# FFN1 by seven block products over two tiles, with Q, K, V plain: one kernel, one core

## The chip, the cores and the metric

The kernel runs on one core of one Trainium2 chip. The metric is the device time of one execution in microseconds; lower is better. The engines are TensorE (PE in the profile, its weight loads PEld), VectorE (DVE), ScalarE (ACT), GpSimd (POOL) and SyncE (SP), which here only issues DMAs. Each engine runs its own instructions in the order in which the built program holds them; semaphores order the engines among themselves.

## The reference

```python
def _A_ref(x, wqkv, wo):                      # S = 2048, D = 576, H = 32, Dh = 18
    qkv = (x @ wqkv).reshape(B, S, 3, H, Dh).transpose(2, 0, 3, 1, 4)
    q, k, v = qkv[0], qkv[1], qkv[2]
    idx = pos[:, None] - off[None, :]         # 8 keys, two apart, behind each position
    mask = idx >= 0
    ...
    logits = jnp.einsum("bhsd,bhswd->bhsw", q, kg) * Dh ** -0.5
    logits = jnp.where(mask[None, None, :, :], logits, -1e9)
    o = jnp.einsum("bhsw,bhswd->bhsd", _softmax(logits, axis=-1), vg)
    return o.transpose(0, 2, 1, 3).reshape(B, S, D) @ wo

def _B_ref(x, w1, b1, w2, b2):                # F = 4608
    h = jnp.einsum("bsd,df->bsf", x, w1) + b1
    r = jnp.where(h > 0, h, 0)
    return jnp.einsum("bsf,fd->bsd", r * r, w2) + b2

xn = _layernorm(A_x, axis=-1)
return A_x + _A_ref(xn, A_wqkv, A_wo) + _B_ref(xn, B_w1, B_b1, B_w2, B_b2)
```

## The kernel before, in words

The 2048 positions are four tiles (`b`) of 512. The model dimension 576 is four chunks of 128 rows and a leftover of 64; the 4608 hidden features are 36 blocks (`f`) of 128. Every factor of a matmul is held as a rounded high part and the difference to it (`split`, L142 to L146: ScalarE writes the high part, DVE the difference), and a product is made of high x high, high x low and low x high. The leftover's two parts are stacked in one chunk of 128 rows.

One loop runs over 144 steps `n`, that is 36 blocks for each tile in turn (`step`). A step loads the weights of a later block, splits the w1 block of the next step (`split_w1`) and its own w2 block (`split_w2`, L149 and L150), runs FFN1 of block `n` (`ffn1`, L698: 14 matmuls of 512 columns into one bank), then ScalarE's relu (L700) and two squares (L703, L704) and DVE's difference (L705), and FFN2 of block `n - 2` (`ffn2`, L723: 14 matmuls into the tile's five output banks). So FFN2 uses activations that were made two steps earlier. At a tile's end the output projection (65 matmuls, also L723) goes into the same banks, and DVE drains them (`drain`, L739) onto the residual.

Around that go, as pieces between the steps: layer norm of the next tile (statistics on DVE, L161 to L169, the inverse root on GpSimd, L170, mean and scale through DRAM by two DMAs named `mr` and `mb`, then L358), Q, K, V, and the attention of eight heads at a time (`attention`): products and sums over DVE (L626, L629), a softmax, and the weighted values, whose sum over the window of eight is three halving additions (L652 to L654). K and V go through DRAM, which shifts them.

Q, K, V of tile 0 are plain matmuls, 14 for each group of 128 rows (L259 in the opening, L404 later). Tiles 2 and 3, and half of tile 1, take them by seven block products over two halves of the rows, the columns and the inner chunks (`multiply`, L586). GpSimd makes the combined weights for that in advance (`preparation`) and passes them through DRAM (`wm`, `we`).

The opening (`open_rows`) loads tile 0 row by row, normalises and transposes it, multiplies its first group of Q, K, V, and goes straight on to FFN1 of block 0. On TensorE, ScalarE, DVE and GpSimd the order of the opening is the order of the code; later the planner of the framework places each engine's instructions, except the last step.

Of the kernel before, what the change touches and what calls it, by code (L numbers as in the profile page):

```python
# [16 lines left out]
P = 128  # L17
# [6 lines left out]
NF = F // P  # L24
G = 4
HG = H // G
CG = HG * DH
HALO = (W - 1) * DIL
# [8 lines left out]
LAG = 2  # L37
WARM = 6
WQ, KV = 512, 2688
WIDE = (448, 512, 384, 384)  # L40
QAT = [sum(n - 2 * CG for n in WIDE[:g]) for g in range(G + 1)]
PAIR = (512, 352)
QP = (0, 448)
PREP = {(1, 0): range(6, 13), (1, 1): (31, 32, 32, 33, 34, 34, 35, 37, 38, 38), (0, 0): range(40, 47), (0, 1): range(51, 61)}
HOME = {(1, 0): "xr", (1, 1): "xb", (0, 0): "xr", (0, 1): "xr"}
OUTS = {}
LEAD = {6: 1, 7: 1, 5: 1, 3: 1}
LN, XT, NORM, RES = {1: 22, 2: 20, 3: 18}, {1: 25, 2: 15, 3: 14}, {1: 12, 2: 9, 3: 11}, {1: 28, 2: 13, 3: 13}
PRODUCTS = {1: {1: range(6, 13)}, 2: {0: range(-6, 1), 1: range(3, 10)}, 3: {0: range(-6, 1), 1: range(3, 10)}}
FETCH = {1: ((2, 14), (3, 18)), 2: ((0, 1), (1, 6), (2, 11), (3, 16)), 3: ((0, 1), (1, 6), (2, 11), (3, 16))}  # L50
PLAIN = {1: ((0, -6, -2), (1, 1, 4))}
# [3 lines left out]
def block_kernel(ctx: ExitStack, tc: tile.TileContext, x, xt, wqkv, wpair, wo, w1, b1, w2, b2, out):  # L55
# [4 lines left out]
    py = ctx.enter_context(tc.tile_pool(name="py", bufs=1, space=bass.MemoryType.PSUM))  # L60
    pw = ctx.enter_context(tc.tile_pool(name="pw", bufs=1, space=bass.MemoryType.PSUM))
# [6 lines left out]
    ident = sb.tile([P, P], F32, name="mb", bufs=1)  # L68
# [6 lines left out]
    zero = sb.tile([PAD, CG], F32, name="pr", bufs=1)  # L75
# [11 lines left out]

    kscr = [dram.tile([PAD + S, CG], F32, name=f"kscr{g}") for g in range(G)]
    vscr = [dram.tile([PAD + S, CG], F32, name=f"vscr{g}") for g in range(G)]

# [3 lines left out]

    oscr = {(b, g): dram.tile([TB, CG], F32, name=f"o{b}{g}") for b in range(NB) for g in range(G)}
    mrscr = {b: dram.tile([2 * NJ, P], F32, name=f"mr{b}") for b in range(1, NB)}

    normed, mb = {0}, {}
    xb, xT, xr, xh, xl, qo, ob, wq = {}, {}, {}, {}, {}, {}, {}, {}
    raw1, raw2, w1s, w2s, hs = {}, {}, {}, {}, {}  # L100
    yp = {}
    turns, held = [0], set()

    def bank(own=False):
        turns[0] += not own
        if own or turns[0] % 3 == 0:
            return pw.tile([P, TB], F32, name="wk")
        return pw.tile([P, TB], F32, name="qk", bufs=2)

    wm = [[dram.tile([P, 4, n], F32, name=f"wm{p}{i}") for i in range(7)] for p, n in enumerate(PAIR)]  # L110
    we = [[dram.tile([P, 2, n], F32, name=f"we{p}{i}") for i in range(3)] for p, n in enumerate(PAIR)]

    def load_x(b, j):
        if b not in xb:
            xb[b] = sb.tile([P, NJ, D], F32, name="xb", bufs=1)
        with tc.issue_after(last_load[0].ins):
            nc.sync.dma_start(xb[b][:, j], xv[b][:, j])

    def load_xt(b):
        xT[b] = sb.tile([P, NC, TB], F32, name="xt", bufs=1)  # L120
        with tc.issue_after(last_load[0].ins):
            nc.sync.dma_start(xT[b], xt[b])

    def load_first():
        xb[0] = sb.tile([P, NJ, D], F32, name="xb", bufs=1)
        raw = sb.tile([P, NC, TB], F32, name="xr", bufs=1)[:, :, :WIDE[0]]
        hi = mt.tile([P, NC, WQ], F32R, name="wqh")[:, :, :WIDE[0]]
# [86 lines left out]
    def open_rows():  # L214
# [13 lines left out]
        def stats(j, *ks):  # L228
            for k in ks:
                bn_stats(0, j, k)  # L230
# [770 lines left out]
```

## Time and profile before

| | before |
|---|---|
| median of three runs | 1150.9 us (1150.66 to 1150.94) |
| span of the profiled execution | 1148.8 us |
| TensorE busy | 1143.9 us, 5167 matmuls |
| DVE busy | 896.9 us |
| ScalarE busy | 598.3 us |
| GpSimd busy | 167.8 us |
| DMA | 244.32 MB, 213 GB/s over the span |

The span goes from the first to the last instruction of one execution taken by the hardware profiler. Rows of groups give line, engine, operation, output <- inputs, shapes and count, then the busy time in us, the mean of one in ns, and the engine's idle time just before them with what ended it. Rows of the chain of waits and of the timeline begin with the start and the length in us. The ends of matmuls are modelled and overlap, so the pitch of matmuls is read from start to start.

### The profile page before, as it was taken

To read this page: it belongs to the slowest core of one execution; us is meant where nothing else is said; L and a number is where in the kernel's file an instruction comes from. 1 tells how busy PE (TensorE), PEld (TensorE's weight loads), DVE (VectorE), ACT (ScalarE), POOL (GpSimd) and SP (SyncE) were. 2 spreads that over 40 slices of the span, in tenths; PEclk is the share of its full clock that TensorE was granted. 3 is DMA by queue.
4 is the path that set the end of the run, shared out by engine and by line. 5 is a ranking of instruction groups with operands and counts; after the bars stand their busy time and mean duration, and the time that the engine had idled before them with its cause. 6 is when DMAs were issued, how large, how long until landed. Compare 5 with 4: busy or idle time off the path is not lost.

```text
span 1148.8 us, 14771 instructions
## 1 busy us (share of the span) xinstructions
PE 1143.9 (100%) x5167; PEld 956.6 (83%) x5167; DVE 896.9 (78%) x1314; ACT 598.3 (52%) x1010; POOL 167.8 (15%) x233
## 2 busy tenths in 40 slices
PE   9999999999999999999999999999999999999998
PEld 7888888888888888888888888888888888888887
DVE  6878898973598999996558899989555989998453
ACT  7646455563545546566335445556543544555652
POOL 2232100012245316420100100000100010000000
PEclk9999999999999999999999999999999999999999
DMA  7749576553679798897578598563667868643421
GB/s 247 247 137 333 141 255 208 151 158 106 227 236 339 224 317 262 272 307 227 181 268 296 184 341 275 144 185 119 192 209 276 283 189 270 216 124 108 133 68 53
DMA packets 102506, 244.32 MB, mean 213 GB/s; under 512 B 14080, under 2 KB 36608, under 8 KB 97184
## 3 DMA queue, kind: packets, MB, share of 16 engines
q1 hardware_dynamic: 86096, 185.20, 50.4%
q0 software_dynamic: 16048, 57.81, 15.7%
q8 instruction: 40, 0.66, 0.2%
q10 hardware_dynamic: 288, 0.38, 0.1%
q14 instruction: 34, 0.28, 0.1%
HBM read 209.34 MB, written 34.00 MB: 212 GB/s over the span
## 4 chain that ended last, share of the span: by engine, by line
PE 99%; DMA 0%; DVE 0%; POOL 0%; issue 0%; POOLq 0%
PE y L723 45%; PE wk L698 20%; PE qk L698 20%; PE qk L586 8%; PE qk L404 3%; PE wk L404 2%; PE qk L259 1%; PE y L195 0%; DMA xb<-in_x 0%; PE wk L259 0%; DVE st L161 0%; PE qk L773 0%; PE wk L773 0%; POOL rs L170 0%; DVE xr L775 0%; DVE xt L189 0%
## 5 line engine op out<-in xcount | busy, mean ns | idle before, releaser
L723 PE MATMUL y<-hh,w2s 128*128 128x512 f32 x1292 | 323.3, 389 | 0.0
L723 PEld LDWEIGHTS y<-hh,w2s 128*128 128x128 f32 x1292 | 242.3, 188 | 49.3
L143 ACT ACTIVATE w1h<-raw 128x640 fp32r<-128x640 f32 x144 | 106.3, 739 | 186.8 <-PE wk L698 102.3
L723 PE MATMUL y<-hl,w2s 128*128 128x512 f32 x718 | 190.3, 389 | 0.0
L145 DVE TENSOR_TENSOR w1l<-raw,w1h 128x640 fp32r<-128x640 f32 x144 | 121.8, 846 | 77.8 <-ACT w1h L143 40.7
L149 ACT ACTIVATE w2s<-raw 128x640 fp32r<-128x640 f32 x144 | 105.8, 737 | 146.1 <-PE y L723 135.7
L723 PEld LDWEIGHTS y<-hl,w2s 128*128 128x128 f32 x718 | 134.7, 188 | 27.6
L150 DVE TENSOR_TENSOR w2s<-raw,w2s 128x576 fp32r<-128x576 f32 x144 | 115.5, 803 | 45.9 <-ACT w2s L149 45.3
L705 DVE TENSOR_TENSOR hl<-r,hh 128x512 fp32r<-128x512 f32 x144 | 103.5, 719 | 31.4 <-ACT r L704 31.0
L698 PE MATMUL wk<-xh,w1h 128*128 128x512 f32 x360 | 106.0, 390 | 0.0
L698 PE MATMUL qk<-xh,w1h 128*128 128x512 f32 x360 | 105.0, 389 | 0.0
L626 DVE TENSOR_TENSOR pr<-qo,kv 128x1152 f32<-128x1152 f32 x64 | 88.8, 1387 | 11.4 <-DMA kv<-kscr 7.6
L703 ACT ACTIVATE hh<-r 128x512 fp32r<-128x512 f32 x144 | 91.0, 632 | 4.9
L698 PE MATMUL wk<-xh,w1l 128*128 128x512 f32 x360 | 93.3, 389 | 0.0
L698 PE MATMUL qk<-xh,w1l 128*128 128x512 f32 x360 | 93.3, 389 | 0.0
L704 ACT ACTIVATE r<-r 128x512 f32<-128x512 f32 x144 | 90.9, 631 | 4.1
L648 DVE TENSOR_TENSOR pr<-lg,kv 128x1152 f32<-128x1152 f32 x64 | 88.7, 1385 | 1.2
L629 DVE TENSOR_REDUCE lg<-pr 128x64 f32<-128x1152 f32 x64 | 86.2, 1347 | 0.1
L698 PEld LDWEIGHTS wk<-xh,w1l 128*128 128x128 f32 x360 | 67.6, 188 | 14.1
L698 PEld LDWEIGHTS qk<-xh,w1l 128*128 128x128 f32 x360 | 67.6, 188 | 14.0
L698 PEld LDWEIGHTS qk<-xh,w1h 128*128 128x128 f32 x360 | 67.6, 188 | 13.9
L698 PEld LDWEIGHTS wk<-xh,w1h 128*128 128x128 f32 x360 | 67.3, 188 | 13.2
(176 smaller groups left out, 1560.1 us busy)
## 6 DMA issues: line engine op xcount, KB each, us to landing
raw<-in_w SPq DMA_DIRECT2D x288, 320.0 KB, 3.7
kv<-kscr SPq DMA_DIRECT2D x10, 1296.0 KB, 7.7
kv<-vscr SPq DMA_DIRECT2D x10, 1296.0 KB, 8.2
wqh<-wm POOLq DMA_DIRECT2D x12, 704.0 KB, 5.7
wqh<-wm POOLq DMA_DIRECT2D x8, 1024.0 KB, 5.8
raw<-in_wo SPq DMA_DIRECT2D x20, 320.0 KB, 3.1
wql<-wm POOLq DMA_DIRECT2D x9, 704.0 KB, 6.9
wql<-wm POOLq DMA_DIRECT2D x6, 1024.0 KB, 5.2
```

Of the source, the lines that this page charges most:

```text
L143: i = nc.scalar.activation(hi, raw, AF.Copy)
L145: i = nc.vector.tensor_tensor(out=lo, in0=raw, in1=hi.bitcast(F32), op=ALU.subtract)
L149: nc.scalar.activation(w[:, :DE], raw, AF.Copy)
L150: nc.vector.tensor_tensor(out=w[:, DE:], in0=raw[:, :D], in1=w[:, :D].bitcast(F32), op=ALU.subtract)
L586: nc.tensor.matmul(qk[t][:, :n], l, r, start=first and c == 0, stop=c == len(mm) - 1, skip_group_check=True)
L626: nc.vector.tensor_tensor(out=pr, in0=q[:, j:j + 1].to_broadcast([P, W, CG]), in1=shifted(k, j, [1, CG]), op=ALU.mult)
L648: nc.vector.tensor_tensor(out=pr.rearrange("p w (a d) -> p w a d", d=DH), in0=at[:, :, :, None].to_broadcast([P, W, HG, DH]), in1=shifted( ...
L698: nc.tensor.matmul(p, l, r, start=i == 0, stop=i == len(mm) - 1)
L703: nc.scalar.activation(hh, r, AF.Square)
L704: last_square[0] = nc.scalar.activation(r, r, AF.Square)
L705: last_hl[0] = nc.vector.tensor_tensor(out=hl, in0=r, in1=hh.bitcast(F32), op=ALU.subtract)
L723: nc.tensor.matmul(yp[b][c], v, a, start=first and c not in cs[:i], stop=c in last and c not in cs[i + 1:], skip_group_check=True)
```

## The change

FFN1 is computed for two tiles and two blocks of features at once. With the tiles `b0`, `b1` as the two rows of a block matrix, the chunks 0 and 1 against 2 and 3 as its inner halves, and the feature blocks 2p and 2p+1 as its columns, the four products that were eight half-products become seven (`ffn_pair`): B11, T1, T2, T3, B21, B22 and T4, each of six matmuls, with eight matmuls for the leftover chunk. T1 to T4 are differences of weight blocks that DVE makes for each pair (`combine_w1`); S1 to S4 are sums of activations that DVE makes once for each pair of tiles (`sums`, `last_sum`). Three banks carry the seven products (a, b, c in the text, `ba`, `bb`, `bc` in the code): ScalarE copies a to b after B11, T2 and T3 add onto b and ScalarE copies b out after each, and DVE adds such a copy to bank c.

The kernel then has four phases after an opening that computes Q, K, V of tiles 0 and 1 (`q0`). Phase A of tiles 0 and 1: 18 pairs of FFN1, with FFN2 of tile 0 (28 matmuls of the pair before) in four groups of seven between the products (`work`); tile 1's activations are written to DRAM (`hscr`), 1 MB a pair. Phase B of tile 1: FFN2 alone, 36 steps, with the activations read back (`load_h`), and the row products of Q, K, V of tiles 2 and 3 between its steps. Then phase A and phase B of tiles 2 and 3. Q, K, V are plain everywhere, 14 matmuls of 432 columns for each of the four groups of heads and each 128 rows. The seven products of Q, K, V, with `preparation` and its DRAM buffers, are gone. Attention's sum over the window is one reduction. TensorE's order is the order of the code throughout; attention is marked as work of low priority (`lazily`) that the planner sets between.

```diff
-    def preparation(p, m):
-    def multiply(b, p, i):
-    def ffn1(n):
...
-            nc.vector.tensor_tensor(out=pr[:, :4], in0=pr[:, :4], in1=pr[:, 4:], op=ALU.add)
-            nc.vector.tensor_tensor(out=pr[:, :2], in0=pr[:, :2], in1=pr[:, 2:4], op=ALU.add)
-            nc.vector.tensor_tensor(out=q[:, j], in0=pr[:, 0], in1=pr[:, 1], op=ALU.add)
+            nc.vector.tensor_reduce(out=q[:, j], in_=pr.rearrange("p w c -> p c w"), axis=AX.X, op=ALU.add)
...
+    def combine_w1(n):
+        r = raw1[n]
+        tt(r[:, T1:T3 + 1], r[:, B12:B22 + 1], r[:, B11:B12 + 1], ALU.subtract)
+        tt(r[:, T2], r[:, B22], r[:, T1], ALU.subtract)
+        tt(r[:, T4], r[:, B21], r[:, T2], ALU.subtract)
+
+    def split_w1(n, k):
+        w1s[n, k] = mt.tile([P, 2, 4, 2 * P], F32R, name="w1s", bufs=3)
+        split(w1s[n, k][:, 0], w1s[n, k][:, 1], raw1[n][:, 4 * k:4 * k + 4])
...
+        def product(to, slot, a, start=False, stop=False, extra=()):
+            mm = []
+            for c in range(2):
+                mm += [(weight(slot, 0, c), a(0, c))]
+            for c in range(2):
+                mm += [(weight(slot, 1, c), a(0, c)), (weight(slot, 0, c), a(1, c))]
+            for f, v in extra:
+                mm += [(weight(LEFT, k, f), v) for k in range(2)]
...
+        def squares(r, name_h):
+            h = mt.tile([P, 2, 2, TB], F32R, name="h", bufs=3)
+            nc.scalar.activation(h[:, 0], r, AF.Square)
+            nc.scalar.activation(r, r, AF.Square)
+            tt(h[:, 1], r, h[:, 0].bitcast(F32), ALU.subtract)
+            return h
+
+        product(ba, B11, A11, start=True)
+        if p == 0:
+            nc.tensor.matmul(bb, weight(B11, 0, 0), A11(0, 0), start=True, stop=True, skip_group_check=True)
+        nc.scalar.activation(bb, ba, AF.Copy)
+        product(bc, T1, ss(1), start=True)
+        work(0)
+        product(bb, T2, ss(2))
+        u = four()
+        nc.scalar.activation(u[:, 0], bb, AF.Copy)
+        left(bc, 1, x4[b1])
+        work(1)
+        product(bb, T3, ss(3))
+        nc.scalar.activation(u[:, 1], bb, AF.Copy)
+        r0, r1 = four(), four()
+        tt(r1[:, 1], bc, u[:, 1], ALU.add)
+        if p + 1 < NP:
+            combine_w1(n + 1)
+            split_w1(n + 1, 0)
+        product(ba, B21, A12, extra=((0, x4[b0]),))
+        relu(r0[:, 0], ba, f0)
+        relu(r1[:, 1], r1[:, 1], f1)
+        work(2)
+        product(bc, B22, S4, extra=((1, x4["d"]),))
+        tt(r0[:, 1], bc, u[:, 0], ALU.add)
+        relu(r0[:, 1], r0[:, 1], f1)
+        hs[n] = squares(r0, 0)
+        product(bb, T4, A22, extra=((0, x4[b1]),))
+        relu(r1[:, 0], bb, f0)
+        work(3)
+        h = squares(r1, 1)
+        nc.sync.dma_start(hscr[s][p], h.rearrange("p k f t -> p (k f t)").bitcast(F32))
+        if p + 1 < NP:
+            split_w1(n + 1, 1)
...
+                ops = pair_products(hs.pop(n - 1), b * NF + 2 * p - 2)
+                ffn_pair(s, p, lambda i: add(b, ops[7 * i:7 * i + 7]))
...
+    def load_h(s, p):
+        t = hs[s, p] = mt.tile([P, 2, 2, TB], F32R, name="h", bufs=3)
+        nc.sync.dma_start(t.rearrange("p k f t -> p (k f t)").bitcast(F32), hscr[s][p])
...
+    YB = {0: (0, 1, 2, 3, 4), 1: (5, 6, 7, 0, 1), 2: (5, 6, 7, 0, 1), 3: (2, 3, 4, 5, 6)}
+    F_BANKS = [(5, 6, 7), (2, 3, 4)]
...
+    def phase_b0():
...
+        for n in range(NF):
...
+            ffn_tile(b, n)
+            if n in GROUPS:
...
+                rows = [(2 + i, g, j) for i in range(2) for j in range(NJ)]
...
+    def q0():
...
+        statistics(1)
+        load_wq(2)
+        load_xt(1)
+        rows(0, 1)
+        split_wq(2, "h")
+        normalize(1)
+        rows(0, 2)
+        load_wq(3)
+        rows(1, 1)
+        split_wq(3, "w1s")
+        sums(0)
+        load_wq(0)
+        rows(1, 2)
+        rows(0, 3)
+        wq.pop(0)
+        split_wq(0, "h")
+        load_w1(0)
+        rows(1, 3)
+        combine_w1(0)
+        split_w1(0, 0)
+        split_w1(0, 1)
+        rows(1, 0)
+        last_sum(0)
```

In `q0`, `rows(b, g)` is four groups of 14 matmuls for tile `b` and group `g` of heads; `statistics(1)` and `normalize(1)` are the layer norm of tile 1, through the same two small DMAs as before.

More of the change, by code (lines that the diff above doesn't have):

```diff
@@ L1 @@
 import math
-from contextlib import ExitStack
+from contextlib import ExitStack, contextmanager
 import concourse.bass as bass
@@ L262, in parts @@
+            nc.tensor.matmul(qp[j][:, :QW], l, (wlo if a == 2 else whi)(c), start=done[j] == 1, stop=done[j] == 3 * NC - 1)
         def parts(j, *which):
```

1235 lines of the change are left out of this document (551 added, 684 removed).

## The prediction

> **What bounds the kernel now.** I read the page first, then the chain of waits, then the groups by line.
>
> ```profile
> span 1148.8 us, 14771 instructions
> PE 1143.9 (100%) x5167; PEld 956.6 (83%) x5167; DVE 896.9 (78%) x1314; ACT 598.3 (52%) x1010; POOL 167.8 (15%) x233
> ...
> PE   9999999999999999999999999999999999999998
> ...
> PEclk9999999999999999999999999999999999999999
> ...
> GB/s 247 247 137 333 141 255 208 151 158 106 227 236 339 224 317 262 272 307 227 181 268 296 184 341 275 144 185 119 192 209 276 283 189 270 216 124 108 133 68 53
> ...
> PE 99%; DMA 0%; DVE 0%; POOL 0%; issue 0%; POOLq 0%
> ```
>
> TensorE is busy in every slice at the full granted clock, and the chain that ended last runs through it for 99%. DVE is busy 78% and ScalarE 52%, all of it behind TensorE. So a change is worth the matmuls that it takes off, less every wait that it puts into TensorE's queue. The busy sum cannot price a matmul, since matmuls overlap; the chain can, by its start-to-start pitch:
>
> ```profile
> 24.29 6.35 PE qk L698 x28
> ...
> 122.67 4.88 PE qk L404 x28
> ...
> 625.02 2.56 PE qk L586 x16
> ```
>
> So 512 columns cost 6.35/28 = 0.227 us, 384 columns 0.174 and 352 columns 0.160; the straight line through 352 and 512 gives 0.193 for 432 and 0.200 for 448. The span is 1148.8; the median of the runs, 1150.9, is 2.1 more. The page gives no other time of the profiled execution, so I make the sum against its span and add 2.1.
>
> **The change, TensorE's work.** FFN1 before: 144 steps of 14 matmuls, 2016. After: 36 pairs of seven products of six plus eight for the leftover rows, 50 each, 1800. 216 x 0.227 = **-49.0 us**; two dummy matmuls, +0.5. FFN2 (2016) and the output projection (260) keep their number. Q, K, V before: tile 0, 56 matmuls at 448, 56 at 512 and 112 at 384, 11.2 + 12.7 + 19.5; tile 1, 112 at 512 and 100 at 352, 25.4 + 16.0; tiles 2 and 3, 200 of each, 45.3 + 32.0; together 162.1. After: 896 of 432 columns, 173.2: **+11.1**. If no wait came in, the span would be 1148.8 - 49.0 + 0.5 + 11.1 = 1111.4.
>
> **The change, in a steady pair.** Before, a step only needed operands made a step earlier. Now three banks are used several times within a pair, and each reuse waits for ScalarE or DVE:
>
> ```profile
> L143 ACT ACTIVATE w1h<-raw 128x640 fp32r<-128x640 f32 x144 | 106.3, 739 | 186.8 <-PE wk L698 102.3
> L145 DVE TENSOR_TENSOR w1l<-raw,w1h 128x640 fp32r<-128x640 f32 x144 | 121.8, 846 | 77.8 <-ACT w1h L143 40.7
> L149 ACT ACTIVATE w2s<-raw 128x640 fp32r<-128x640 f32 x144 | 105.8, 737 | 146.1 <-PE y L723 135.7
> ...
> L150 DVE TENSOR_TENSOR w2s<-raw,w2s 128x576 fp32r<-128x576 f32 x144 | 115.5, 803 | 45.9 <-ACT w2s L149 45.3
> L705 DVE TENSOR_TENSOR hl<-r,hh 128x512 fp32r<-128x512 f32 x144 | 103.5, 719 | 31.4 <-ACT r L704 31.0
> ...
> L626 DVE TENSOR_TENSOR pr<-qo,kv 128x1152 f32<-128x1152 f32 x64 | 88.8, 1387 | 11.4 <-DMA kv<-kscr 7.6
> L703 ACT ACTIVATE hh<-r 128x512 fp32r<-128x512 f32 x144 | 91.0, 632 | 4.9
> ...
> L629 DVE TENSOR_REDUCE lg<-pr 128x64 f32<-128x1152 f32 x64 | 86.2, 1347 | 0.1
> ```
> ```profile
> 1000.28 2.20 PE L723 MATMUL y<-hh,w2s 128*128 128x512 f32 x9
> 1000.48 0.69 ACT L700 ACTIVATE r<-qk,b1t 128x512 f32<-128x512 f32 x1 [0.39 <-PE qk L698]
> ...
> 1001.87 0.63 ACT L704 ACTIVATE r<-r 128x512 f32<-128x512 f32 x1
> ...
> 1002.53 0.69 DVE L705 TENSOR_TENSOR hl<-r,hh 128x512 fp32r<-128x512 f32 x1 [0.38 <-ACT r L704]
> ```
>
> The timeline gives the hand-overs: ScalarE starts 0.20 after TensorE has gone on to its next group, DVE 0.03 after ScalarE ends; I take 0.05 for all but TensorE's. A read of PSUM at 512 wide costs ScalarE 0.69. No row has 1024 columns: by 632 ns at 512 and 739 at 640 a ScalarE pass of 1024 is 1.06 us; its bounds are 0.74 (the 640-wide row) and 1.26 (two of 512). DVE at 1024 is 1.26 between the rows of 512 and 1152.
>
> I walk one pair with the order in which the built program puts its instructions. Zero is the end of product T3. TensorE, never waiting: B21 (8 matmuls) to 1.81, seven of FFN2 to 3.40, B22 to 5.21, T4 to 7.03, seven to 8.61, then the next pair's B11 to 9.97, T1 to 11.33, seven to 12.92, T2. T2 may start only when ScalarE has copied bank a to bank b. Most pairs have this order on ScalarE: second copy of bank b, 0.89; w1 split, 1.95; two relus, 3.27; then it stands, because the next relu needs DVE's sum after B22: 5.41 to 6.10. Behind it, in order: that relu, 6.78; square, 7.84; relu, 8.53; w1 split, 9.59; w2 split, 10.33; square, 11.39; square, 12.45; w2 split, 13.19; and only now the copy, 13.88. TensorE stands from 12.92 to 13.9: **1.0 us** of each pair. In other pairs the first square comes after a relu of T4's result and both w2 splits; it ends at 12.2 where TensorE wants it at 11.33, and the copy at 13.9 again. Few orders give less (0.4) or more (1.6). DVE has an attention instruction of 1.35 to 1.39 ahead of its sum in about half of the pairs, ending some 0.3 late: I take 1.15. 34 pairs: **+39 us**. Bounds: 0 if ScalarE keeps up; 2.4 a pair (82) if each sum waits out a whole attention instruction.
>
> DVE itself: a pair costs two sums at 0.70, the weight combinations (one of 512 columns, two of 256 at some 0.48, below the 288-wide row that follows: 1.7), four passes of 1024 and two w2 differences at 0.80, 9.8 us, and attention stands in between. The 17 intervals of the first phase sum to 292 us, 17.2 each, under the pair's 78 x 0.227 = 17.7, and well under 18.8 with the wait. So DVE does not bind.
>
> The attention's last step replaces three additions by one reduction over w that reads every 144th element.
>
> ```profile
> L626 DVE TENSOR_TENSOR pr<-qo,kv x64: 1299/1352/2502, 32.9 to 1034.9; 128x1152 f32<-128x1152 f32 x64
> ```
> ```profile
> L652 DVE TENSOR_TENSOR pr<-pr 128x576 f32<-128x576 f32 x64 | 51.5, 804 | 0.4
> ...
> L653 DVE TENSOR_TENSOR pr<-pr 128x288 f32<-128x288 f32 x64 | 31.8, 497 | 1.1
> L654 DVE TENSOR_TENSOR qo<-pr 128x144 f32<-128x144 f32 x64 | 24.9, 388 | 1.3
> ```
>
> Before: 1.69 us. After: no row reads with such a stride, so I bound it by the reduction of as many contiguous elements, 1.35, and by the slowest instruction over 1152 elements in the trace, 2.50 (the largest of the first row above), and take 1.35, the nearest row. Here the Trainium skill speaks against the change: "Advanced Engine Details and Errata", section "SBUF Cachelines", says that reads which go to a new 16-byte line each time pay a penalty, without a figure. By that rule the second rival's time would come out; the trace of before has no such read that could agree or not.
>
> **The change, at the opening.** Before, FFN1 of tile 0 starts as soon as its rows are there. Now 28 further row products, of tile 1 too, come first, and TensorE's order is fixed.
>
> ```profile
> 14.92 0.56 POOL L170 TENSOR_TENSOR rs<-rs,half 128x1 f32<-128x1 f32 x1 [1.72 <-DVE rs L169]
> ...
> 15.76 0.87 ACT L187 ACTIVATE xt<-xb,nm,rs 128x576 f32<-128x576 f32 x1 [0.45 <-DVE nm L180]
> ...
> 20.74 0.36 PE L259 MATMUL qk<-wql,xh 128*128 128x448 f32 x1
> ```
> ```profile
> kv<-kscr SPq DMA_DIRECT2D x10, 1296.0 KB, 7.7
> ```
> ```profile
> mr<-mr SPq DMA_DIRECT2D x1, 4.0 KB, 11.0
> ```
> ```profile
> mb<-mr SPq DMA_DIRECT2D x3, 512.0 KB, 7.2
> ```
> ```profile
> L358 DVE TENSOR_TENSOR xt<-xt,mb x30: 681/684/693, 225.3 to 793.2; 128x512 f32<-128x512 f32 x30
> ```
> ```profile
> L161 DVE BATCH_NORM_STATS2 st<-xb 128x6 f32<-128x288 f32 x32 | 12.6, 444 | 1.8 <-DMA xb<-in_x 1.8
> ...
> L165 DVE BATCH_NORM_AGGREGATE mv<-st 128x2 f32<-128x12 f32 x16 | 2.8, 192 | 0.1
> ...
> L169 DVE TENSOR_SCALAR mr<-mv 128x1 f32<-128x1 f32 x12 | 1.6, 143 | 0.0
> ...
> L210 DVE TENSOR_TENSOR xh<-y,r 64x128 fp32r<-64x128 f32 x4 | 1.2, 295 | 0.2
> ```
>
> Tile 1's rows go into a buffer that is free when the last rows of tile 0 are normalised, 16.6; with 7.7 (the 1296 KB row, the nearest) they land at 24.4. In DVE's built order the first statistic of tile 1 stands ahead of the last piece of tile 0, and seven more ahead of the first weight difference of group 1 (864 columns, 1.1 by the step from 512 to 640): 24.4 + 8 x 0.44 + 0.3 + 1.1 = 29.3. TensorE, at some 20.9 with all that it can do, waits **8**. Then on DVE three more weight differences (1.1, 0.6, 1.1), a combination (0.7) and twelve short instructions (4 x 0.19 + 8 x 0.14) end at 34.7; the power on GpSimd and the issue, 35.8; 11.0 for the 4 KB of means and 7.2 to spread them, 54.0. Normalising takes six passes of 1024 and three of 512, 9.6, with three of attention between them, 4.1: 67.7. TensorE has two groups of four rows to do, 8 x 14 x 0.193, and is through at 51, at some 53 with tile 1's first row, which now ends at 68: **15** more. Bounds: 10 together (rows landed at 21, a spread in half the time) and 30.
>
> The first pair of a phase has no FFN2 to cover it. In the first phase ScalarE's copy of T2 stands behind an exponential of attention that waits for DVE, 2.0 by DVE's queue; B22 waits 0.4 for the first sum, and the next pair's FFN2 1.9 for a square behind five DVE instructions: 4. In the second, without the exponential, 3. Together **7**.
>
> **Ends and the rest.** Tile 1's FFN2 takes over two banks of tile 0, and tile 3's two of tile 2:
>
> ```profile
> L739 DVE SCALAR_TENSOR_TENSOR xr<-y,b2t,xr 128x512 f32<-128x512 f32 x14 | 9.7, 746 | 2.4 <-PE y L723 2.2
> ```
>
> Two drains before the first bank, one more before the second, less three matmuls: 1.8 each, **3.6**. The pairs' second activations go out as 1 MB and come back: a pair of FFN2 steps needs 1.05 + 2 x 0.33 MB in 6.35 us, 268 GB/s, which slices of the page exceed (341). GpSimd's weight preparations and most of their queue go:
>
> ```profile
> q0 software_dynamic: 16048, 57.81, 15.7%
> ```
>
> They ran behind TensorE, which never waited for them, so nothing is gained; without that cover they would be worth their part of 168 us of POOL. Sum: 1111.4 + 23 + 7 + 39 + 3.6 = 1184; with 2.1, **1186**.
>
> **The rivals.** (1) *ScalarE keeps up.* Place: the copy before T2. From the second sum to the copy ScalarE has four passes of 1024; at 0.83 us instead of 1.06 the copy ends at 12.9 and the wait is gone. For it: ScalarE has only 12.6 us of work in 17.7. Against: the 640-wide row alone is at 0.74, and it cannot pass the relu it waits at. Time: 1186 - 39 = 1147, just faster; with half of the opening's wait too, 1135.
> (2) *DVE becomes the bound.* Place: the strided reduction, from some 2.3 us on (292 + 28 x 0.97 = 17 x 18.8). At 2.50, the 28 of the first phase make its 292 us 324, 19.1 a pair, and late sums add to ScalarE's wait: with 0.5 to 1.1 more a pair, 1203 to 1223. For it: nothing strided in the trace shows it free.
> (3) *The way through DRAM binds.* If DMA gives only the 247 GB/s of the opening, a pair of FFN2 steps takes 6.9 instead of 6.35: 36 x 0.55 = 20, 1206. Against: the 341.
> (4) *Seven products cover as intended* and the opening too: 1113.5. Against it both walks.
>
> **How the numbers follow.** Forecast 0.62; (1) 0.17; (2) 0.12; (3) 0.05; (4) 0.04. About 0.2% is what a measurement of this kernel can tell from no change. (2) and (3) are slower; of (1) and (4), 0.03 lies within 0.2%: faster 0.18, same 0.03, slower 0.79. The forecast alone, with the opening's and the pairs' bounds drawn in to half: 1160 to 1212. The range takes in (2) and most of (1): 1138 to 1225.
>
> **What would show it.** A pair's start-to-start near 18.8 us in both phases A, with TensorE's idle before T2 released by ScalarE's PSUM copy; a gap of some 8 us near 21 and of 15 near 53, released by DVE; 512-wide pitch still 0.227; FFN2-only stretches without gaps; the strided reduction at 1.35. Pairs at 17.7, or TensorE at 99% again, would refute it.

## The result, and the profile after

The changed kernel takes 1232.0 us (median of four runs, 1230.2 to 1234.4) against 1150.9 before: a ratio of 1.0707, with a 95% interval of 1.0692 to 1.0722. It is slower, as forecast, but by 81 us where 35 were forecast, and lies 7 us above the range. The profiled execution of after, again as the first part of its page:

```profile
span 1230.7 us, 13553 instructions
PE 1142.7 (93%) x5013; PEld 945.1 (77%) x5013; DVE 933.2 (76%) x1074; ACT 575.1 (47%) x809; POOL 18.3 (1%) x32
...
PE   8499697999999999999999968999999999999998
...
PEclk9899898999999999999999988999999999999999
...
PE 35%; DVE 33%; DMA 13%; issue 9%; ACT 7%; SPq 2%; POOL 0%; DVEq 0%; ACTq 0%; POOLq 0%
```

TensorE has holes now, its clock is below full speed in several slices, and the chain that ended last runs through it for 35% where it was 99%. The holes by what ended them, from the view of waits, TensorE alone (us in total, times, longest):

```profile
PE p L368 <- ACT p L387: 19.1, 14, 8.9
PE p L368 <- DVE r L103: 15.5, 12, 5.0
PE p L250 <- ACT X L107: 15.2, 1, 15.2
PE p L331 <- ACT w1s L107: 11.0, 1, 11.0
```

L387 is ScalarE's copy from bank a to bank b, L103 on `r` is DVE's sum that bank c waits for, `X` is tile 1's normalised rows, `w1s` on L331 are the weights' buffers that the output projection of tile 1 uses. I set each stretch against its matmuls at full pitch (512 columns 0.2266 us, and 432 columns 0.1958, since 266 matmuls of the rows start between 67.51 and 119.59; the prediction's line gave 0.193):

| stretch | matmuls at full pitch | taken | more |
|---|---|---|---|
| opening with Q, K, V of tiles 0, 1 | 448 x 0.1958 = 87.7 | 119.6 | 31.9 |
| first phase A, with the projection | 1470 x 0.2266 = 333.1 | 380.2 | 47.1 |
| phase B of tile 1 | 569 x 0.2266 + 448 x 0.1958 = 216.7 | 235.2 | 18.5 |
| second phase A | 333.1 | 358.5 | 25.4 |
| last phase | 569 x 0.2266 = 128.9 | 137.3 | 8.4 |

Three windows show what the pairs share with DVE. The columns are the window, its length, the busy times of TensorE, its weight loads, DVE, ScalarE and GpSimd with their instructions, the granted clock, and the DMAs' share and GB/s:

```profile
149.40:466.70 317.30, 295.65 (x1250) 235.94 (x1249) 295.92 (x323) 182.21 (x245) 3.12 (x4) 0.98 0.54 180
...
760.00:952.30 192.30, 182.76 (x782) 146.62 (x781) 184.92 (x197) 115.55 (x156) 0.00 (x0) 0.99 0.48 170
952.30:1060.30 108.00, 107.56 (x469) 87.50 (x468) 52.55 (x61) 66.85 (x90) 0.00 (x0) 1.00 0.40 140
```

In the first two, attention runs on DVE, and DVE is busy for 93% and 96% of the time; the pairs take 19.8 and some 19.2 us. In the third attention is over, DVE is half idle, and six pairs take 108.0 / 6 = 18.0. A pair's 78 matmuls are 17.67. Of DVE's time each of the 16 pairs in the first window has 295.92 / 16 = 18.5 us, which is more than TensorE's 17.67.

One of the waits for DVE, near 360 us, as ScalarE, DVE and TensorE have it:

```profile
356.96 0.60 ACT L396 ACTIVATE r<-p 128x512 f32<-128x512 f32 x1 [2.80 <-PE p L368]
...
356.32 2.19 DVE L288 TENSOR_REDUCE q<-pr 128x144 f32<-128x1152 f32 x1
358.39 1.25 DVE L103 TENSOR_TENSOR h<-r,h 128x1024 fp32r<-128x1024 f32 x1
359.53 0.46 DVE L103 TENSOR_TENSOR w1r<-w1r 128x256 f32<-128x256 f32 x1
359.86 1.39 DVE L103 TENSOR_TENSOR pr<-lg,kv 128x1152 f32<-128x1152 f32 x1
361.13 0.72 DVE L103 TENSOR_TENSOR r<-p,r 128x512 f32<-128x512 f32 x1
...
361.91 1.65 PE L368 MATMUL p<-X,w1s 128*128 128x512 f32 x6 [1.59 <-DVE r L103]
```

The sum `r<-p,r` needs ScalarE's copy (L396), which ends at 357.56. It starts at 361.13, 3.6 us later, because two instructions of attention (2.19 and 1.39 us), the difference of an activation and a combination of weights stand ahead of it in DVE's order; TensorE, which needs bank c for B22, stands for 1.59 us.

### The profile page after: what moved, and what is told of

Same layout as the page of the kernel before. It is cut to its first block, busy times and chain, and to the rows that moved or that the text cites. A ratio compares the mean times of both kernels' runs of the same rounds, so it can differ in the third digit from the quotient of the medians.

```text
span 1230.7 us, 13553 instructions
## 1 busy us (share of the span) xinstructions
PE 1142.7 (93%) x5013; PEld 945.1 (77%) x5013; DVE 933.2 (76%) x1074; ACT 575.1 (47%) x809; POOL 18.3 (1%) x32
## 4 chain that ended last, share of the span: by engine, by line
PE 35%; DVE 33%; DMA 13%; issue 9%; ACT 7%; SPq 2%; POOL 0%; DVEq 0%; ACTq 0%; POOLq 0%
PE p L331 21%; PE p L368 9%; DVE q L288 7%; DVE pr L103 7%; DMA w1r<-in_w 5%; PE p L250 4%; DVE h L103 3%; DMA q<-qscr 3%; DVE w1s L103 3%; DVE w2s L103 3%; DVE lg L272 3%; DVE r L103 2%; DVE w1r L103 2%; ACT w2s L113 2%; ACT h L379 2%
## 5 line engine op out<-in xcount | busy, mean ns | idle before, releaser
L331 PE MATMUL p<-h,w2s 128*128 128x512 f32 x2010 | 488.4, 392 | 14.3 <-ACT h L379 4.4
L331 PEld LDWEIGHTS p<-h,w2s 128*128 128x128 f32 x2010 | 378.5, 189 | 99.7 <-ACT h L379 9.1
L368 PE MATMUL p<-X,w1s 128*128 128x512 f32 x864 | 224.9, 397 | 15.2 <-DVE r L103 15.1
L103 DVE TENSOR_TENSOR w2s<-w2r,w2s 128x576 fp32r<-128x576 f32 x164 | 123.4, 755 | 137.7 <-ACT w2s L113 136.5
L113 ACT ACTIVATE w2s<-w2r 128x640 fp32r<-128x640 f32 x164 | 120.3, 736 | 200.4 <-PE p L331 133.5
L368 PEld LDWEIGHTS p<-X,w1s 128*128 128x128 f32 x864 | 163.8, 191 | 54.9 <-DVE r L103 20.9
L368 PE MATMUL p<-S,w1s 128*128 128x512 f32 x648 | 171.9, 402 | 22.8 <-ACT p L387 19.1
L368 PEld LDWEIGHTS p<-S,w1s 128*128 128x128 f32 x648 | 121.7, 191 | 58.6 <-ACT p L387 29.5
L250 PE MATMUL p<-w1s,X 128*128 128x432 f32 x576 | 123.1, 363 | 19.6 <-ACT X L107 15.2
L288 DVE TENSOR_REDUCE q<-pr 128x144 f32<-128x1152 f32 x64 | 139.5, 2179 | 0.5
L103 DVE TENSOR_TENSOR pr<-q,kv 128x1152 f32<-128x1152 f32 x64 | 86.6, 1354 | 16.8 <-DMA q<-qscr 16.4
L103 DVE TENSOR_TENSOR h<-r,h 128x1024 fp32r<-128x1024 f32 (+2 forms) x78 | 92.0, 1198 | 9.6 <-ACT r L380 6.5
L103 DVE TENSOR_TENSOR w1s<-w1r,w1s 128x1024 fp32r<-128x1024 f32 x72 | 87.9, 1221 | 10.6 <-ACT w1s L107 10.6
L103 DVE TENSOR_TENSOR r<-p,r 128x512 f32<-128x512 f32 x72 | 49.6, 688 | 50.9 <-ACT r L396 26.7
L103 DVE TENSOR_TENSOR pr<-lg,kv 128x1152 f32<-128x1152 f32 x64 | 87.0, 1359 | 1.0
L103 DVE TENSOR_TENSOR w1r<-w1r 128x256 f32<-128x256 f32 (+1 forms) x108 | 55.1, 510 | 33.2 <-DMA w1r<-in_w 32.1
```

Of the source, the lines that this page charges most:

```text
L103: return nc.vector.tensor_tensor(out=out, in0=a, in1=b, op=op)
L113: nc.scalar.activation(w[:, :DE], raw, AF.Copy)
L250: nc.tensor.matmul(p[:, :QW], l, r, start=k == 0, stop=k == len(mm) - 1)
L288: nc.vector.tensor_reduce(out=q[:, j], in_=pr.rearrange("p w c -> p c w"), axis=AX.X, op=ALU.add)
L331: nc.tensor.matmul(yp[b][c], v, a, start=c not in yb[b], stop=c in last and c not in [o[0] for o in ops[i + 1:]], skip_group_check=True)
L368: nc.tensor.matmul(to, l, r, start=start and i == 0, stop=i == len(mm) - 1, skip_group_check=True)
```

## The experiments

All times are medians; a kernel is compared with after (1232.0 us, 1.0707) or with the kernel that it is built on. The theory that I tested against the forecast's own (ScalarE's order costs each pair the same) was that DVE, filled by attention, brings the sums and weight differences late.

**The strided reduction undone.**

```diff
-            nc.vector.tensor_reduce(out=q[:, j], in_=pr.rearrange("p w c -> p c w"), axis=AX.X, op=ALU.add)
+            tt(pr[:, :4], pr[:, :4], pr[:, 4:], ALU.add)
+            tt(pr[:, :2], pr[:, :2], pr[:, 2:4], ALU.add)
+            tt(q[:, j], pr[:, 0], pr[:, 1], ALU.add)
```

> The attention's last step is three halving additions again, as before the change. DVE theory (the pairs of phase A are late because DVE, filled without a pause by attention, brings the two sums and the w1 differences late): 2.18 us become about 1.69, 28 x 0.49 = 14 us less in the first phase A, some 20 x 0.49 = 10 us less in the second; DVE is busy there for 296 of 317 and 185 of 192 us, so most of it shows: 1205 to 1215 us. ScalarE theory (the forecast: the order on ScalarE ahead of T2 costs every pair about the same): the pairs stay, 1228 to 1235 us.

The groups by shape, of after and then of this kernel (count, busy us, mean ns, idle before):

```profile
L288 DVE TENSOR_REDUCE q<-pr 128x144 f32<-128x1152 f32 x64 | 139.5, 2179 | 0.5
...
L272 DVE TENSOR_REDUCE lg<-pr 128x64 f32<-128x1152 f32 x64 | 86.4, 1350 | 0.7
```
```profile
L103 DVE TENSOR_TENSOR pr<-pr 128x576 f32<-128x576 f32 x64 | 48.2, 753 | 0.8
...
L103 DVE TENSOR_TENSOR pr<-pr 128x288 f32<-128x288 f32 x64 | 29.0, 453 | 0.9
...
L103 DVE TENSOR_TENSOR q<-pr 128x144 f32<-128x144 f32 x64 | 19.5, 305 | 1.1
```

1203.5 us, 28.5 less. The reduction of contiguous elements beside it takes 1.35 us, the strided one 2.18; the three additions take 1.51 together. The steady pairs (the 16 intervals behind the first) fell from 317 to 302 us in the first phase A and from 300 to 292 in the second; most of the rest came from the second phase's first pair, 20.8 to 14.9. That is DVE's theory, and more than its estimate.

**Attention without its arithmetic.**

```diff
-        lg = sb.tile([P, NA, W], F32, name="lg")
...
-            nc.vector.tensor_reduce(out=q[:, j], in_=pr.rearrange("p w c -> p c w"), axis=AX.X, op=ALU.add)
+        for t in (k, v):
+            tt(q[:, 0, :8], q[:, 0, :8], t[:, 0, :8], ALU.add)
```

> Leaves out the arithmetic of attention (products, sums, softmax) and keeps its loads and its store, so DVE has nothing but FFN work in phase A. DVE theory: all pairs come at the 18.07 us that the last pairs of the second phase A show, 16 x (19.8 - 18.07) = 28 and 16 x (18.76 - 18.07) = 11 us less, the first pairs lose most of their 12 and 8, the opening some 4: about 1175 us. ScalarE theory: pairs stay near 18.8, about 1215 us.

1204.5 us. The pairs did what DVE's theory says: 18.1 each in both phases, but for two behind the first pairs and the last of each phase. The time did not: the first pair still took 16.2 us to its mark (the two leftover matmuls behind T2), so its wait is not DVE's arithmetic, and in this kernel's other order the wait ahead of tile 1's output projection was 21.5 us. So 18.1 instead of 17.7 is what a pair costs without DVE, and two waits had still no cause.

**A strided write in place of the strided read.**

```diff
-            pr = sb.tile([P, W, CG], F32, name="pr")
+            pr = sb.tile([P, CG, W], F32, name="pr")
...
-            nc.vector.tensor_reduce(out=q[:, j], in_=pr.rearrange("p w c -> p c w"), axis=AX.X, op=ALU.add)
+            nc.vector.tensor_reduce(out=q[:, j], in_=pr, axis=AX.X, op=ALU.add)
```

> The weighted values are written with a stride of 8 elements so that the last reduction reads contiguous elements. If only strided reads cost: the reduction falls from 2.18 to 1.35 us and the product stays at 1.36; by the DVE theory then 1195 to 1212 us, by the ScalarE theory 1228 to 1235. If a strided write costs like a strided read: the product rises to about 2.2, DVE's sum stays, 1228 to 1236 by either.

The same groups of this kernel:

```profile
L103 DVE TENSOR_TENSOR pr<-lg,kv 128x1152 f32<-128x1152 f32 x64 | 153.8, 2404 | 1.0
...
L288 DVE TENSOR_REDUCE q<-pr 128x144 f32<-128x1152 f32 x64 | 86.3, 1348 | 0.5
```

1241.3 us. The reduction is at 1.35, but the product that writes every eighth element went from 1.36 to 2.40: a stride costs where it is written, too, and a little more.

**The row groups of phase B earlier.**

```diff
-    GROUPS = {8: 0, 15: 1, 22: 2, 29: 3}
+    GROUPS = {4: 0, 11: 1, 18: 2, 25: 3}
```

> In the FFN2 phase of tile 1 the groups of Q, K, V rows of tiles 2 and 3 start four steps earlier, so that the buffer st, which they share with the regrouped attention of tile 1, is free before the phase ends. Theory of the shared buffer: the 11.0 us wait ahead of the output projection of tile 1 goes, with some 1 us at half clock behind it: 1219 to 1222 us. Rival, SP's queue: the 16 issues of 0.64 us are late anyway, 1228 to 1233 us.

1244.7 us, slower than either theory had it. The wait ahead of the projection was still 7.9 us at 718, and the first rows now waited 6.7 us at 519 for their normalised tiles. What stood ahead of the projection was SP, as its own timeline in after shows:

```profile
702.78 0.58 SPq L460 DMA_DIRECT2D st<-o  x1
703.46 0.54 SPq L467 DMA_DIRECT2D w2r<-in_wo  x1
704.05 1.86 SPq L460 DMA_DIRECT2D st<-o  x3
705.96 1.30 SPq L467 DMA_DIRECT2D w2r<-in_wo  x1
707.30 7.59 SPq L460 DMA_DIRECT2D st<-o  x12
```

Sixteen DMAs regroup tile 1's attention into `st`, at 0.64 us each, behind the last store out of `st` and between weight loads that wait for their buffers.

**The regroup earlier.** On top of the three additions:

```diff
-    GROUPS = {8: 0, 15: 1, 22: 2, 29: 3}
+    GROUPS = {8: 0, 14: 1, 20: 2, 26: 3}
...
             if n == 30:
+                regroup(b, 0)
                 regroup(b, 1)
...
-        regroup(1, 0)
```

> On top of the three additions (1203.5 us): the groups of Q, K, V rows in the FFN2 phase of tile 1 start every six steps and end at step 29, and the 16 DMAs that regroup the attention of tile 1 stand at step 30 in the code and not behind the phase's last w2 loads. Queue theory (SP issues them in order, 0.64 us each, behind a w2 load that waits for its buffer): the 11 us wait ahead of the output projection goes, and the half clock behind it: 1189 to 1193 us. Rival (the attention of tile 1 itself ends too late, or the wait only moves as it did when the rows alone were moved): 1200 to 1206 us.

1197.8 us, between the two: the wait went from 10.8 us with the three additions alone to 3.9, no further; in its trace the sixteen still stand among weight loads.

**ScalarE's order.** Two kernels on top of the three additions. In the first the second w2 split of a pair was only written behind the copy L387 in the code; in the second it is tied to it (`pay` is the split that is owed from the pair before):

```diff
-        nc.scalar.activation(bb, ba, AF.Copy)
+        i = nc.scalar.activation(bb, ba, AF.Copy)
+        with tc.issue_after(i.ins):
+            pay()
...
-                split_w2(b * NF + 2 * p + f)
+                split_w2(b * NF + 2 * p + f, f == 0 or p + 1 == NP)
```

> On top of the three additions (1203.5 us): the split of a pair's second w2 block, 0.63 us of ScalarE, stands behind the copy of bank a to bank b instead of ahead of it. ScalarE theory for what is left in a quiet pair (18.1 instead of 17.7 us): the copy comes 0.63 earlier, quiet pairs take 17.7, 32 x 0.4 = 13 us less: 1189 to 1194 us. Rival (DVE's lateness alone counts, and the copy waits anyway): 1200 to 1205 us.

> As the kernel with the second w2 split written behind the copy, but now tied to it, so that ScalarE's order really changes (there the planner had put the split ahead of the copy again). On top of the three additions (1203.5 us). ScalarE theory: the copy ends 0.63 us earlier, quiet pairs take 17.7 instead of 18.07, the pairs that DVE holds up gain less: 1189 to 1198 us. Rival (something else releases T2): quiet pairs stay at 18.07, 1200 to 1206 us.

The first took 1204.2 us: its planner put the split ahead of the copy all the same, so it says nothing. The second took 1194.8, 8.7 less than the three additions alone. ScalarE in a quiet pair of after, and the same stretch with the split behind the copy (L399 there), TensorE's rows below each:

```profile
1016.05 0.72 ACT L375 ACTIVATE r<-r,b1t 128x512 f32<-128x512 f32 x1 [3.21 <-DVE r L103]
1016.81 1.06 ACT L379 ACTIVATE h<-r 128x1024 fp32r<-128x1024 f32 x1
1017.77 0.67 ACT L375 ACTIVATE r<-p,b1t 128x512 f32<-128x512 f32 x1
1018.34 1.05 ACT L107 ACTIVATE w1s<-w1r 128x1024 fp32r<-128x1024 f32 x1
1019.29 0.72 ACT L113 ACTIVATE w2s<-w2r 128x640 fp32r<-128x640 f32 x1
...
1021.82 0.72 ACT L113 ACTIVATE w2s<-w2r 128x640 fp32r<-128x640 f32 x1
1022.45 0.58 ACT L387 ACTIVATE p<-p 128x512 f32<-128x512 f32 x1
...
1021.24 1.75 PE L331 MATMUL p<-h,w2s 128*128 128x512 f32 x7
1023.09 1.65 PE L368 MATMUL p<-S,w1s 128*128 128x512 f32 x6
```
```profile
981.11 0.58 ACT L399 ACTIVATE p<-p 128x512 f32<-128x512 f32 x1
981.62 1.36 ACT L113 ACTIVATE w2s<-w2r 128x640 fp32r<-128x640 f32 x2
...
981.16 1.75 PE L343 MATMUL p<-h,w2s 128*128 128x512 f32 x7
982.74 1.52 PE L380 MATMUL p<-S,w1s 128*128 128x512 f32 x6
```

In after, seven matmuls start at 1021.24 and T2 only 1.85 later, where 7 x 0.2266 = 1.59 would do; with the split behind the copy it is 1.58. Quiet pairs went from 18.07 to 17.7. So the forecast's wait is real, of its cause and at its place. In the profiles the 32 steady intervals lost 13.5 us (593.6 to 580.1); the first interval of each phase became longer, 19.8 to 26.0 and 14.9 to 18.6. In the first, DVE stood 8.9 us for a w1 load that came 2.5 us behind the small DMA `mr` and took 13.4 us to land, a wait that the runs on `mr` below explain; for the second no run shows the cause.

**An addition on GpSimd.** On top of the three additions, the first of them:

```diff
-            tt(pr[:, :4], pr[:, :4], pr[:, 4:], ALU.add)
+            nc.gpsimd.tensor_tensor(out=pr[:, :4], in0=pr[:, :4], in1=pr[:, 4:], op=ALU.add)
```

> On top of the three additions (1203.5 us): the first of them, 128x576, goes to GpSimd, which is idle. DVE theory: 64 x 0.8 = 51 us less on DVE; the pairs of the first phase A go from 302 towards the 289 us of the kernel without the softmax, those of the second from 292 to 290, with some of the waits around them: 1186 to 1192 us. Rival (GpSimd holds DVE up, or its slower addition makes attention late): 1203 us or more.

From this kernel's view of waits:

```profile
DVE pr L103 <- POOL pr L288: 32.5, 23, 1.6
```

1233.5 us, 30 more. The addition takes GpSimd 1.75 us, DVE stands 32.5 us in its order for it, and DVE's own 1024-wide differences of w1 became slower beside it, from a mean of 1.22 us to 1.38: the 19 of them that overlap one of GpSimd's additions take 1.81 on the average, the other 53 still 1.22. What is off DVE's sum is not off its path.

**TensorE kept busy in its longest wait.** After, with 88 matmuls that nothing reads ahead of tile 1's first rows:

```diff
+        fp = bank(r[0] % 8)
+        for _ in range(88):
+            nc.tensor.matmul(fp[:, :QW], X[0][:, 0, 0, :P], wq[2][0][:, 0, 0], start=True, stop=True)
         load_wq(3)
         rows(1, 1)
```

> The changed kernel, with 88 matmuls of 432 columns put into TensorE's wait for tile 1's rows (17.3 of 18.4 us), whose results nothing reads. Clock theory (the half clock follows TensorE's idleness): the rows behind the wait come at the full pitch of 0.197 us instead of 0.36 to 0.39, the half clock of 49.9 to 66.9 us is gone: 2.0 us less, 1229 to 1231 us. Rival (the half clock has another cause): 1231 to 1233 us and 0.36 again.

TensorE's timeline behind the wait, of this kernel and then of after:

```profile
46.22 17.40 PE L836 MATMUL p<-h,X 128*128 128x432 f32 x88
63.76 2.58 PE L250 MATMUL p<-w1s,X 128*128 128x432 f32 x12
```
```profile
63.13 4.15 PE L250 MATMUL p<-w1s,X 128*128 128x432 f32 x11 [2.31 <-DVE X L103]
```

Behind the filled wait twelve matmuls take 2.58 us; in after eleven took 4.15. The clock theory holds. The filling ran 0.6 us over, so the opening itself was only 0.2 shorter; the 4 us by which the kernel is faster (1227.8) came mostly in the first phase A, and I do not count them for the clock.

**And without the loads of K and V.**

```diff
-        k, v = (sb.tile([P, NE, CG], F32, name="kv", bufs=3) for _ in range(2))
...
-        for t, n in ((k, "k"), (v, "v")):
-            nc.sync.dma_start(t.rearrange("p e c -> p (e c)"),
...
+        tt(q[:, 0, :8], q[:, 0, :8], q[:, 0, 8:16], ALU.add)
```

> Leaves out the arithmetic of attention and its loads of K and V (32 DMAs of 1296 KB); its load of Q and its store stay. DMA theory of the opening and the first pair (w1 of the second pair takes 14.6 us to land, 4.0 elsewhere, because K and V are loaded beside it): the first pair comes to its mark in 5 to 8 us instead of the 16.2 of the kernel that keeps the loads, and tile 1's rows come some 4 to 8 us sooner; together 1180 to 1195 us. Rival (the w1 load is late by its buffer or by SP's order alone): the first pair stays above 13 us, 1198 to 1206 us.

1188.4 us, but it did not separate the two theories: the first pair came to its mark in 8.2 us, and the next interval was 16.3 where 12.9 are due. So I read, in after, SP's timeline around the late load, DVE's row that waited for it, and the view of the DMAs between 170 and 200 us (KB each, median us to landing):

```profile
112.12 0.55 SPq L156 DMA_DIRECT2D mr<-mr  x1
113.08 0.70 SPq L295 DMA_DIRECT2D w1r<-in_w  x1
```
```profile
127.70 0.69 DVE L103 TENSOR_TENSOR w1r<-w1r 128x512 f32<-128x512 f32 x1 [10.60 <-DMA w1r<-in_w]
```
```profile
w1r<-in_w SPq DMA_DIRECT2D x1, 640.0 KB, 14.2
mr<-mr SPq DMA_DIRECT2D x1, 4.0 KB, 12.5
```

In that later window the same two DMAs stand together again. Both late w1 loads are those issued right behind `mr`, which writes 1024 single elements of 4 bytes; a w1 load takes 4.0 us in the median.

**The means written in rows.** After, with the 4 KB of means and scales turned on DVE first:

```diff
...
-        nc.sync.dma_start(mrscr[b].rearrange("n p -> p n"), mr.rearrange("p k j -> p (k j)"))
+        nc.vector.transpose(mt_, mr)
+        for i in range(G):
+            nc.sync.dma_start(mrscr[b][:, i * L:(i + 1) * L], mt_[i * L:i * L + 2 * NJ])
```

> The changed kernel, with the means and scales of a tile (4 KB) turned on DVE in blocks of 32 first and written by four DMAs in pieces of 128 bytes, where one DMA wrote 1024 elements of 4 bytes. Theory of the small elements (the w1 loads of the first phase A that take 14 us to land are those issued right behind that DMA, at 113 and 179 us, and wait for its elements): w1 lands in 4 to 6 us everywhere, the first pair comes to its mark in 5 to 8 us instead of 14.75, the pair of 27.3 us takes 18 to 20, the opening is some 6 us shorter: 1205 to 1214 us. Rival (K and V beside it make w1 late): 1228 to 1234 us, the w1 loads at 14 again.

The view of this kernel's DMAs, from 100 to 135 us:

```profile
w1r<-in_w SPq DMA_DIRECT2D x3, 640.0 KB, 6.0
```

1202.7 us, 29.3 less than after. Of the three w1 loads between 100 and 135 us the trace has one landing, 6.0 us after the issue, with a 1296 KB load of V issued next to it; DVE stands 2.9 us for it, where it stood 10.6. The first pair takes 6.6 us to its mark instead of 14.75, the interval of 27.3 is 18.7, the opening 113.0 instead of 119.6. The small elements held what was queued behind them. The w1 load is issued 3.9 us after the last of the four here and 1.0 after `mr` in after, but that is not the cause: with the three additions alone a w1 load issued 8.3 us after `mr` still took 10.0. Whether the larger pieces helped or the four DMAs in place of one, no run tells.

**The parts together.** The additions, the regroup and the tied split, and tile 0's fourth group ahead of tile 1's rows; then the means in rows too:

```diff
-        normalize(1)
         rows(0, 2)
         load_wq(3)
-        rows(1, 1)
-        split_wq(3, "w1s")
+        split_wq(3, "S")
+        rows(0, 3)
+        normalize(1)
+        rows(1, 3)
...
-        rows(1, 3)
+        rows(1, 1)
```

> Three additions, the regroup early and the w2 split behind the copy, and in the opening the 56 matmuls of the fourth group of tile 0 stand ahead of tile 1's first rows (its weights go into the buffers that later hold S1 to S3). If tile 1's rows come when they came before (67 us): TensorE has 11 us more to do, its wait goes from 18.4 to about 7.4 us: 1176 to 1186 us. Rival (the earlier loads of that group's weights crowd the DMAs, and the means and tile 1's rows come later by as much): 1187 to 1197 us.

> The kernel with tile 0's fourth group first (1179.7 us) and the means written in pieces of 128 bytes. Small elements: its pairs of 21, 23 and 30 us in the first phase A come down to 18 to 19, 16 to 20 us less there, and some 4 in the opening: 1156 to 1164 us. Rival (K and V, as above): 1177 to 1182 us.

From the page of the second:

```profile
span 1152.3 us, 13655 instructions
...
PEclk9999999999999999999999999999999999999999
```

1179.7 and 1155.9 us (1.0049 of before, 1.0034 to 1.0063). The small elements were also worth 24 us here, though attention and the w1 loads had moved. Its clock is at 0.9 of full speed or more in every slice. Four more kernels tried the waits left, with these edits. The first kernel has the first two, and the row groups one step earlier; the second has the third edit besides. The third has the first edit, and the second for tiles 2 and 3 alone; the fourth has the last edit besides.

```diff
+        nc.gpsimd.tensor_tensor(out=mr[:, NJ:2 * NJ], in0=mr[:, NJ:2 * NJ], in1=half, op=ALU.pow)
...
-                nc.sync.dma_start(t[g * L:(g + 1) * L].rearrange("l (j i) c -> l i j c", i=G)[:, i],
+                (nc.sync, nc.gpsimd)[i % 2].dma_start(t[g * L:(g + 1) * L].rearrange("l (j i) c -> l i j c", i=G)[:, i],
...
+        with tc.issue_after(last_act.ins), tc.issue_after(last_dve.ins):
             q0()
...
+        with tc.issue_after(kept_dma[1, 0].ins):
             residual(1)
```

> On top of the kernel with all parts (1155.9 us): one power on GpSimd for a tile's four scales instead of four of 1.4 us each (DVE stands 6 us at 104 us for them), the regroup's DMAs issued by SP and GpSimd in turn, and the row groups one step earlier. If these waits are what is left: 3 us in the first pairs, 4 to 6 ahead of the output projection of tile 1 and behind it, 1 to 2 at the start of the last phase: 1145 to 1150 us, so below the kernel before. Rival (they are covered, or only move): 1153 to 1157 us.

> The same, and tile 1's statistics stand behind the split of the first group's weights on DVE, so that TensorE's first wait (2.2 us at 20.7, with 1.8 at half clock behind it) goes: 3 to 4 us less than the kernel beside it if tile 1's rows still come in time; no less if the rows of tile 1, 2.6 us later, give it back at 58 us.

> The kernel with all parts mended (1155.9 us), with one power on GpSimd instead of four, and half of the regroup's DMAs issued by GpSimd for tiles 2 and 3 only; the phase of tile 1 stays as there. By the phases of the runs before: 4 us less in the last phase, 1 to 2 in the first: 1149 to 1152 us, level with the kernel before. Rival (the 4 us belong to the earlier row groups): 1154 to 1157 us.

> The same, and the 1 MB load of tile 1's residual stands on SP behind the DMAs of the regroup, which the output projection waits for. DMA theory of that wait (4.7 us at 657, with a w2 load of 7 us in the chain at some 400 GB/s): 2 to 5 us less than the kernel beside it, 1145 to 1149 us, below the kernel before. Rival (SP's 16 issues set it): no less.

They took 1157.6, 1163.3, 1154.9 and 1158.1 us. Only the third has a median below 1155.9, and its runs spread from 1150.2 to 1161.8. With GpSimd issuing half of the regroup the last phase went from 138.3 to 133.7 us in the third kernel. In the first two, phase B of tile 1 became longer, 227.5 to 234.7, with that queue and the earlier row groups together. The later statistics of the second made the opening longer, 102.8 to 108.3; the later residual of the fourth left phase B at 227.0 (226.5 in the third). No version beat the kernel before: the best is at 1.0036 of it (1.0019 to 1.0052).

## Why the prediction missed

The sign held; most of the terms did not. Measured are the waits of after with the half clock behind each:

| term | forecast | measured |
|---|---|---|
| Q, K, V plain | 11.1 | 13.3 (0.1958 a matmul) |
| opening waits | 23 | 22.3 |
| first pairs of both phases A | 7 | 20.4 |
| steady pairs | 39 | 52.1 |
| ends of the phases | 3.6 | 5.7 |
| ahead of tile 1's projection, and a step before | 0 | 14.2 |
| start of the last phase, for w2 | 0 | 2.2 |

The difference, 46.5, is the miss (1230.7 - 1184 = 46.7).

- **The opening** came as walked in its sum, not in its parts, so that 22.3 stands beside 23 is luck: tile 1's rows landed at 18.6, not 24.4, so the first wait was 2.2 and not 8; TensorE then reached tile 1's rows sooner and waited 18.2 there. Their first matmul came at 60.1 and the rest from 63.1; the first row ended at 67.5, where 68 was forecast.
- **The pairs: the step that failed is "So DVE does not bind"**, and under it "take 1.35, the nearest row" for the strided reduction. It takes 2.18, inside the bounds that I had set and near the upper one. The rest of DVE's sum was right: with 25 of these reductions in the 16 pairs of the first window, 0.83 us each is 1.3 a pair, from the forecast's 17.2 to the 18.5 measured. That is over TensorE's 17.67, so DVE binds already by its sum. By my own rival (2) it should bind only from 2.3; that threshold compared DVE with a pair of 18.8, which held ScalarE's wait of 1.15. Against the 18.07 of the quiet pairs the same sum gives 1.9 (292 + 28 x 0.54 = 17 x 18.07; an estimate). The pairs' 19.8 lies above 18.5 still, and that I put down to DVE's order, as in the rows at 357: a sum that is due stands behind whole instructions of attention. With the three additions, where DVE is busy for 278.49 / 16 = 17.4 a pair (between 145.4 and 447.3 us), the pairs still took 18.9. Taking 0.67 us off each of 64 instructions gave 28.5 us (the three additions). What the Trainium skill says ("Advanced Engine Details and Errata", "SBUF Cachelines": reads that go to a new line each time pay) agrees with this trace, 2.18 against 1.35. I weighed that rival at 0.12.
- **ScalarE's order** was the right mechanism, mis-sized: 0.4 us a pair and not 1.15. I added durations; the rows above start 0.95 apart where one lasts 1.05, so the nine passes from the relu at 1016.05 to the end of the copy take 6.98 us where I had 7.78. The Trainium skill states this overlap, about 93 ns ("ScalarE: Activation LUTs", "What ACT_TABLE_LOAD costs"); the trace agrees with 0.10. So of the 52.1 of the steady pairs some 32 x 0.4 = 13 are the wait that I forecast (the tied split took 13.5 off these intervals), and the rest is DVE's: that my 39 is no further off is luck.
- **The first pairs** were priced by what DVE and ScalarE do. I had quoted the `mr` row and used it only as a latency in its own chain; I did not ask what is queued behind it. It holds the next w1 load to 14 us, at 113 and at 179 us: 29.3 us in all when it was mended, the opening's 7 among them. The second phase's first pair has another cause: its 20.8 us to the next mark became 21.4 with the means in rows and 14.9 with the three additions, and TensorE's wait in it, 5.0 us, ends with DVE's sum.
- **Ahead of tile 1's projection** I had no term. The regroup's buffer is shared with the row groups that the change moved into that phase, and SP's sixteen issues come after it. That SP's order set the rest is argued from its timeline and from the wait going from 10.8 to 3.9; to the end it wasn't settled.
- **The clock** was taken as constant, as before's rows show it. Here it halves after waits, some 17 us in all, by half the time of the 82 matmuls that start in such stretches; it is in the measured column.
- **Rival (3)** did not come: FFN2 of the phases B never waited for activations read back, and the 512-wide pitch stayed at 0.227. FFN1 did get its 49 us off TensorE; none of it reached the end.

## What to carry to other kernels

A busy share of DVE under 100% is no proof that it doesn't bind: set its time per pair against TensorE's matmuls alone, not against a pair that already holds waits. Where TensorE waits for a short instruction in DVE's queue, price the instructions that can stand ahead of it. A strided operand cost 1.6 to 1.8 times a contiguous one here. For each DMA ask what is queued behind it and in how many pieces it writes: three writes of 4 KB in single elements cost more here than the 36 MB of activations that went to DRAM and back. And once TensorE waits about 2 us, add the half clock that follows.

## What the runs showed of the hardware that I had not expected

**The half clock.** Three windows of after (columns as above), one at full clock for comparison, then one with a wait of 2.3 us from 165.9 and the one behind it:

```profile
135.20:138.60 3.40, 3.40 (x16) 2.78 (x16) 3.25 (x5) 1.55 (x2) 0.00 (x0) 1.00 0.21 53
165.90:169.30 3.40, 1.17 (x5) 0.99 (x6) 3.40 (x7) 3.15 (x5) 0.00 (x0) 1.00 0.72 212
169.30:172.70 3.40, 3.40 (x10) 2.69 (x9) 3.40 (x8) 0.60 (x1) 0.00 (x0) 0.51 0.89 341
```

TensorE is busy throughout the last, at a clock of 0.51, with 10 matmuls where full clock does 15 or 16. The clock records change on a grid of 3.413 us. Cut on that grid, over after and the seventeen experiments, every one of 94 windows at full clock with 2.03 us or more of idle TensorE was followed by one at half clock, 17 of 25 with 1.8 to 2.03 us, 3 of 205 with 0.8 to 1.8 us, and none with less. The Trainium skill ("TensorE: Matmul & The Clock Gate", "Why this matters for your kernels") allows gaps up to about 3 us. Here 2 us in one window were enough, and not always in one piece: 1.56 and 0.64 us in one window, in the second of the last four kernels, were followed by half clock too.

**Strides on DVE.** 128x1152 elements with a stride of 576 bytes: 2.18 us read, against 1.35 contiguous; with one of 32 bytes: 2.40 us written, against 1.36.

**Small elements.** In after one DMA of 1024 elements of 4 bytes took 9.8 to 12.5 us. A 640 KB load of w1, 4.0 us in the median, took 13.4 to 16.1 us in after and five other kernels when it was issued up to 2.5 us behind that DMA, and 10.0 to 12.0 us in six kernels when it came 4.6 to 9.6 us behind. With four DMAs of 128-byte pieces in its place the three such loads whose landing the traces have took 4.0 to 6.2 us; how long the four took themselves, the traces do not show.
